# Windowed attention on one core: crossed projection stripes, one-bank reads, 192-byte copies of x, and 14 or 13 units in turn on VectorE

## The chip, the cores and the metric

The kernel runs on one core of a Trainium2 chip. The metric is the device time of one execution in microseconds (us). Times of the kernel before: median 968.16 us of 3 runs (967.62 to 971.61).

## The reference, cut to what matters

The input is an image x of 224 x 224 positions with 96 channels in bf16. It is multiplied with one weight to q, k and v. The first 48 channels attend inside horizontal stripes of 8 rows, the last 48 inside vertical stripes of 8 columns. Both parts go through one output weight.

```python
qkv = jnp.einsum('bhwc,cd->bhwd', x, wqkv)            # 96 -> 3 * 96
q, k, v = qkv[..., :C], qkv[..., C:2 * C], qkv[..., 2 * C:]
scale = C2 ** (-0.5)                                  # C2 = 48, sw = 8
qh = q[..., :C2].reshape(B * nh, sw * W, C2)          # 28 stripes of 1792 positions
...
ah = _softmax(jnp.einsum('bqc,bkc->bqk', qh, kh) * scale, axis=-1)
oh = jnp.einsum('bqk,bkc->bqc', ah, vh)
...                                                   # the same by columns: av, ov
return jnp.einsum('bhwc,cd->bhwd', o, wo)             # o = oh in channels 0..47, ov in 48..95
```

## The kernel before, in words

Two stripes are worked on together; such a pair is called P. Pairs 0 to 13 are horizontal, 14 to 27 vertical. Of the two stripes one (w = 0) lies in partitions 0 to 63 of every tile and the other (w = 1) in 64 to 127. TensorE's array is used as four corners of 64 x 64: a matmul that reads partitions 0 to 63 and writes partitions 64 to 127 uses another corner than one that reads and writes 0 to 63.

**Units.** The 1792 queries of a pair are cut into chunks of 512, 512, 512 and 256 (CH). For each chunk the 1792 keys are gone through in units: a unit has 128 keys and 512 queries, or 256 keys and 256 queries in the last chunk. So a pair has 14 + 14 + 14 + 7 = 49 units. For a unit, `qk` (L752) makes the scores of both stripes in two PSUM banks, reading and writing the same half of the partitions. Then the exponential is taken in one of two ways:

- on ScalarE (`add_a`, L791): one ACTIVATE over both banks, 1024 columns, to a PT buffer; the two banks have to be neighbours;
- on VectorE (`add_d`, L809): one TENSOR_SCALAR over both banks writes 16-bit integers whose bits, read as bf16, are a coarse exponential (I_sb). Two units share a buffer. Usually two shifted copies are added (U_sb and E_sb, L825), on GpSimd or, where the order says `u`, on VectorE, and the three together correct the coarse form. One group in each pair (QUAD, the sixth, two units) is corrected by masks and a product instead (L813, L814 on VectorE; G_sb, L818, on GpSimd, or on VectorE where the order says `p`).

`ndc` and ND = ["4432"] say how many units of each chunk go to VectorE: 4, 4, 3 and 2, which is 13 of 49; 36 go to ScalarE.

`pv` (L775) multiplies the weights with V, which carries columns of ones, so that the sum of the weights comes along. One product for a ScalarE unit, three for a VectorE unit, two in the corrected group. It writes the other half of the partitions than it reads (`at`), and so uses the two corners that `qk` leaves alone. A chunk collects in one PSUM bank and is then copied to OT_sb on VectorE (L846).

**Projection.** `fin` multiplies OT_sb with the output weight, in groups of up to five blocks. In horizontal pairs (L664, groups in HB) it reads one half and writes the other, as `pv` does. In vertical pairs (L694, groups in VB) both matmuls of a step read the same half of OT_sb, and write both halves. VectorE takes the reciprocal of the sums (L649) and multiplies; horizontal results are kept in Ph_sb (L669), vertical ones go to tmp (L698), are added to Ph_sb on GpSimd (L703), and 16 stores a pair bring them out (`added`, SyncE).

**Loading x.** `blocks` (L407) copies a pair's part of x inside HBM to `x_blocks`, in runs of 64 channels (128 bytes), four copies a pair: two halves of the channels times two stripes. `load` (L414) then transposes it into xa_sb and xb_sb by two DMA transposes, and `prep` makes q, k and v of the next pair (L525, L605). The copies of pairs 1, 2 and 3 are issued at the start; in pair P follow the copies for P + 4 and the transposes for P + 2. All of these DMAs are issued from SyncE.

**The order.** It is written out by hand, outside the kernel's loops. Each operation is put into a stream with a letter (`wk.add`), and the string SEQ says letter by letter which stream's next operation comes: A an exponential on ScalarE, a and b scores, c, d and D products with V, j a read on VectorE, f and e the next pair's projection and its evacuations, g and r those of the output, o the copy to OT_sb, U and P work of GpSimd, u and p the same on VectorE, X and x the copies and loads of x, y a store. BANK gives the PSUM bank of each new tile in the same way. `Work.run` walks SEQ and notes each operation's semaphore waits; `emit` writes each engine's part of it in that order.

Of the kernel before, what the change touches and what calls it, by code (L numbers as in the profile page):

```python
# [19 lines left out]
ND = ["4432"]  # L20
QUAD = [(5,)]
SIDE = [""]
# [6 lines left out]
def diag(P, c):  # L29
    return str(c) in SIDE[P % len(SIDE)]  # L30


SEQ = (
    "HiIxIihIiHiIhiiiihIiHXiiihIiiIixhhxhhxhxhxihxHhxihhhHhxhhhxehHhxehHhxHfexeeaaxaeAbbxajbbAxccfxjbccbXaajbUAXbXj"
    "acacaAaUefAefacacebAcbcuaadadjcAaVcfAeaacUbcbAdacjacddAbdbdadaudadAjfVacccAdbdbedadjadadAbcaxDDDbADaDjaUDaDDAa"
    "oddbcbcAdaxjdaUddAdadadbdbAgajcaccUAcadaxdrdbrAbdxadjadaDxDAUcaccxcbAbcacxjacacADaxDfDtDAaxDaDefcUcxcAefcacace"
    "fAaodddaUdeAdadadefdtDAacacaecPacADaDfDdaAkcefPccceffAcfcadaucaeAgkacPcrcrfffADaDefffkcaegaAcacrcracXcAcaPcbbo"
    "ddAdadajVddAgbbDDrDjXbbDVccacacjAcacacUccArbcbgodXdajacacXAacUcdXrbdrAdbdaXjdadgAXdaUdaDrDbrAbDDajcacfAccaUcac"
    "ebdAXbddajdadfAdacacUecbDAbDaDjaDfcXAcacacUeXcaAcacbXboddAdadXjadfdUdAdadaedbDAbeDaDajDfcAkcaUdadedaAdacbgbcAc"
    "jcaUdadcAacraDrbDbDAcajcaUDfcAcacaecfcAcaceacfkcfAtcaaaodddfkAdadefdfdfAdaeDaDbDbtAgacacjPcADacaccrcaArUgbcard"  # L40
# [24 lines left out]
    "DjaccAUaaodddbdbADaXDjaDfDAdXUdacaecXAbcbcacjaXcfcAacUaccegAaraodddbrdAbdadajUdadAdadfDDaADegbDacUrcbArcacajdf"
    "dAdadacecaUAdaegbdrDbrDAacacjfDDAckacakcekcbAbcacjacacAcacaccuaAbboddUddAjdadaDaDAdagbdbrDUArdadaDjcacAcacfddA"
    "uadadbdebdAcajcaccfADaDaDeDacaAcbtcbcfjcfAcfcacacAceaUaccaaodAddadatdfdfAdbpdbDfDAjDaPDaccAcaegaUcrcArffcfacaX"
    "cePgaAcbrcarbDDAdVajdacccAcacaXcbubcAcajacVccAacaoddbdAbdaDjaDfXDAUdadaXDecbAcbXcacjacfcXAcUacacegAacaroddadAr"
    "dadbUdbgAdjadaddDADarDarUDbcbAcajcacfdAcacaceUcbAbdadjadfdAdcacaDeaDAUaDebDbcfcAjcacaccAcakecUagcrcAarabodddbd"
    "AdajdakdfdkAdadaDeDbAbDaDjacfcUcAcadaedadAadbDbgDAjUcacaddAcarcarDaDaAccbtcbcfjcfAcacacfcAcaeUcacaaAoddadadtdf"  # L70
    "AdfdfpdaDaADbeDPbDcjAfcfcacaUcfAceXgacacrbdPrbAdacajgcAacVaccrcArcaXcabDubDAcacajcaVcAcacoddbdAbdXaDjaDfDAXUda"
    "daceXcbADbcacXjacfcAcUcaacegAcaarodddrfAdadaUdbedbADaDjaDfDdAdadaecbUcbAecacjagcAdadadrdbrkAdbUdajDaDfDAcaDace"
    "acAcakcbugbcAcarcjkaccAccacarcacaAbUoddbddAjdadadfdADaDeaDUbDbAdadjacfccAdadaedbUdbAcagjaddAcacacrcarADDatDbDb"
    "AfcftcacacfjcAPcaacccAecaPaccaaAoddadadPdfAdfdfdbebcAUDaDjaDfDfcfAacPaXcedadAacbgbuccrAjcVaacccAcarcaXgUcArcar"
    "caDbDAcbacjacccVAcaaXodddbAdbXDajDadfAUdXaDaDceXbcAbcacjacfcAcUacaccegAaaoddadrdaArgUdbdrdbrAdadjadfDADaDaDecb"
    "UcAbcacjacfcAdadadedaAUacebcbdfdAjDDaDaDAckcaeUgacbcrAbcracacjcAcacackacUAaoddbdbdjdAadadfddAkdaegaDDrArfDaDac"
    "efcfAUcfcaedadbAdbdajdadDAffUcacacfcaAeDaDbDbcfAjcaccacffAcaXceacactacAbcbctAodddaPdadjdAdaXgadVDArDarDaDbcbcA"
    "caucajcPcAcaXcacacAagXpbdbdrcXuAcajcaVcXDAcacarDbcbcAUacjacaccAaodddbdbADaDjaDfUDAdadacecbAcbcajaccfcAUacacceg"
# [106 lines left out]
class Work:  # L185
# [63 lines left out]
    def emit(s, eng, name):  # L249
        known = {}  # L250
        for waits, op in s.out[name]:
# [9 lines left out]
            op.fn(eng).then_inc(op.wait[0], 16 if op.dma is not None else 1)  # L261


HB = [0, 5, 10, 15, 20, 24, 28]
VB = [0, 5, 10, 14]


def bass_standalone__window_attn_cswin__vision_kernel(
# [8 lines left out]
    SW = 8  # L277
# [633 lines left out]
```

## Time and profile before

The profiled execution took 970.69 us. Its span is 968.9 us, the rest lies around it.

| | before |
|---|---|
| median of 3 runs | 968.16 us |
| profiled execution / its span | 970.69 / 968.9 us |
| mean granted clock of TensorE | 0.996 |
| GpSimd busy | 724.3 us, 75% |
| DMA, mean over the span | 65 GB/s |
| HBM read, written | 25.32 MB, 34.41 MB |

In the lines of the profile, PE is TensorE's matmuls, PEld its weight loads, DVE VectorE, ACT ScalarE, POOL GpSimd and SP SyncE, whose DMA issues stand as SPq. L775 is line 775 of the kernel. A group's line has the operation, output<-input with shapes, how often, then busy us and mean ns of one, then the idle time ahead of it and what ended it. A timeline's line has the start, the length, the operation and how many of it are merged; in brackets stands idle time and what ended it. The name behind "waited for" is the instruction whose end released the waiting one.

### The profile page before, as it was taken

The numbers are of one execution on the slowest core, as the hardware profiler recorded it, in microseconds if no ns is written. First come the engines' busy times: TensorE is split into PE (matmuls) and PEld (weight loads), VectorE is DVE, ScalarE is ACT, GpSimd is POOL, SyncE is SP. The second block draws the span as 40 slices with busy tenths as digits, with TensorE's granted clock in tenths as the row PEclk, the third lists the DMA queues.
The fourth block names the chain that finished last, engine by engine and source line by source line (L and its number), as shares of the span: only waits on it lengthen the run. The fifth ranks groups of instructions, "written<-read, shape, count | busy, mean of one in ns | idle before, by whom it ended". The sixth has DMA issues, their size and how long they took to land.

```text
span 968.9 us, 46993 instructions
## 1 busy us (share of the span) xinstructions
PE 956.6 (99%) x21130; PEld 651.4 (67%) x21130; DVE 893.7 (92%) x1426; ACT 942.6 (97%) x1017; POOL 724.3 (75%) x537
## 2 busy tenths in 40 slices
PE   8999999999999999999999999999999999999997
PEld 4667666767666676667677766777776677667674
DVE  7789999999899999999989999999999999999994
ACT  6989999999999999999999999999999999999996
POOL 4778768767966867887778787878777877777772
PEclk9999999999999999999999999999999999999999
DMA  7965234414541553355135345435652631231102
GB/s 120 164 106 79 32 49 79 70 21 71 78 69 14 78 73 46 42 79 79 38 44 80 73 65 79 80 60 85 97 92 47 84 68 33 45 65 32 29 14 50
DMA packets 355098, 63.22 MB, mean 65 GB/s; under 512 B 354784, under 2 KB 354784, under 8 KB 354896
## 3 DMA queue, kind: packets, MB, share of 16 engines
q1 hardware_dynamic: 353312, 59.67, 40.1%
q8 instruction: 165, 2.70, 1.2%
q10 hardware_dynamic: 1584, 0.55, 0.2%
q14 instruction: 37, 0.30, 0.1%
HBM read 25.32 MB, written 34.41 MB: 62 GB/s over the span
## 4 chain that ended last, share of the span: by engine, by line
PE 97%; DVE 2%; ACT 1%; issue 1%; ACTq 0%; DVEq 0%
PE ps L775 51%; PE ps L752 33%; PE ps L525 5%; PE ps L605 4%; PE ps L694 2%; PE ps L664 1%; DVE I_sb L809 1%; ACT PT L791 1%; PE ps L388 0%; DVE KT_sb L545 0%; DVE out_sb L708 0%; PE ps L486 0%; DVE U_sb L813 0%; DVE tmp L698 0%; DVE E_sb L814 0%
## 5 line engine op out<-in xcount | busy, mean ns | idle before, releaser
L791 ACT ACTIVATE PT<-ps 128x1024 bf16<-128x1024 f32 x1008 | 938.5, 1039 | 12.0 <-PE ps L752 8.5
L752 PE MATMUL ps<-QT_sb,KT_sb 48*64 48x512 bf16 (+1 forms) x6272 | 762.4, 357 | 3.7 <-issue 2.0
L775 PE MATMUL ps<-PT,V_sb 64*50 64x512 bf16 (+1 forms) x4592 | 517.2, 351 | 0.0
L809 DVE TENSOR_SCALAR I_sb<-ps 128x1024 int16<-128x1024 f32 x364 | 444.5, 1222 | 31.0 <-PE ps L752 18.1
L752 PEld LDWEIGHTS ps<-QT_sb,KT_sb 48*64 48x64 bf16 x6272 | 275.0, 105 | 164.3 <-ACT PT L791 62.0
L775 PEld LDWEIGHTS ps<-PT,V_sb 64*50 64x50 bf16 x4592 | 238.7, 100 | 39.7 <-ACT PT L791 0.5
L825 POOL TENSOR_SCALAR U_sb<-I_sb 128x2048 int16<-128x2048 int16 (+1 forms) x121 | 213.3, 1763 | 63.8 <-DVE I_sb L809 37.8
L825 POOL TENSOR_SCALAR E_sb<-I_sb 128x2048 int16<-128x2048 int16 (+1 forms) x126 | 224.5, 1782 | 42.6 <-PE ps L775 18.9
L775 PE MATMUL ps<-U_sb,Vs_sb 64*50 64x512 bf16 (+1 forms) x1344 | 195.4, 359 | 0.0
L775 PE MATMUL ps<-I_sb,V_sb 64*50 64x512 bf16 (+1 forms) x1344 | 190.0, 360 | 0.2
L775 PE MATMUL ps<-E_sb,Vs_sb 64*50 64x512 bf16 (+1 forms) x1344 | 175.7, 359 | 0.0
L703 POOL TENSOR_TENSOR out_sb<-tmp,Ph_sb 128x480 bf16<-128x480 f32 (+1 forms) x84 | 85.8, 1027 | 32.0 <-DVE tmp L698 9.4
L818 POOL TENSOR_TENSOR G_sb<-I_sb,U_sb 128x512 bf16<-128x512 bf16 x58 | 66.0, 1154 | 46.6 <-DVE E_sb L814 34.4
L620 POOL TENSOR_SCALAR Vs_sb<-V_sb 128x1400 bf16<-128x1400 bf16 x56 | 76.0, 1358 | 22.3 <-DVE U_sb L825 5.6
L775 PEld LDWEIGHTS ps<-U_sb,Vs_sb 64*50 64x50 bf16 x1344 | 73.7, 100 | 18.6
L846 DVE CAST OT_sb<-ps 128x512 bf16<-128x512 f32 x112 | 69.4, 619 | 15.5 <-PE ps L775 14.0
L775 PEld LDWEIGHTS ps<-E_sb,Vs_sb 64*50 64x50 bf16 x1344 | 71.9, 100 | 14.0
L775 PEld LDWEIGHTS ps<-I_sb,V_sb 64*50 64x50 bf16 x1344 | 68.4, 100 | 14.8 <-ACT PT L791 1.2
L525 PE MATMUL ps<-xa_sb,w_sb 48*64 48x512 bf16 (+3 forms) x440 | 77.5, 351 | 0.1
L525 PE MATMUL ps<-xb_sb,w_sb 48*64 48x512 bf16 (+2 forms) x436 | 75.8, 349 | 0.0
L539 DVE TENSOR_SCALAR QT_sb<-ps 128x512 bf16<-128x512 f32 (+1 forms) x111 | 68.5, 618 | 3.0 <-PE ps L525 1.4
L545 DVE TENSOR_SCALAR_CACHE_REDUCE KT_sb<-ps 128x512 bf16<-128x512 f32 x110 | 67.6, 617 | 0.9 <-PE ps L525 0.8
(66 smaller groups left out, 918.4 us busy)
## 6 DMA issues: line engine op xcount, KB each, us to landing
x_blocks<-in_x_dram SPq DMA_DIRECT2D x106, 224.0 KB
out_dram<-out_sb SPq DMA_DIRECT2D x208, 42.0 KB, 2.1
out_dram<-out_sb SPq DMA_DIRECT2D x22, 24.0 KB, 1.9
xa_sb<-x_blocks SPq DMA_TRANSPOSE x27, 5.1
xb_sb<-x_blocks SPq DMA_TRANSPOSE x27, 5.4
Ph_sb<-in_x_dram ACTq DMA_DIRECT2D x1, 336.0 KB, 3.2
x_blocks<-in_x_dram SPq DMA_DIRECT2D x2, 168.0 KB
out_dram<-out_sb ACTq DMA_DIRECT2D x6, 24.0 KB, 1.9
```

Of the source, the lines that this page charges most:

```text
L525: ins = e.matmul(out_, lhsT=wt, rhs=rhs, start=i == 0, stop=startup or i == 1)
L539: return e.tensor_scalar(dst, src, QS, None, ALU.mult)
L545: return e.tensor_scalar(dst, src, 1.0, None, ALU.mult, ALU.add, accum_out=acc)
L620: vs_ready.setdefault(P, []).append(wk.add("V", Op("pool", 1.4, lambda e, i=i: e.tensor_scalar(Vs_sb[b][i][:, :, :].rearrange("p k c -> p ...
L703: return lambda e, bk: e.tensor_tensor(out_sb[b][:, k0:k1, w, :], tmp[t][:, s0:s1, :], Ph_sb[:, k0:k1, j0 + w, :], ALU.add)
L752: ins = e.matmul(bank(t.k)[64 * w:64 * w + 64, i * qs:(i + 1) * qs], lhsT=KT_sb[b][64 * w:64 * w + C2, 64 * k:64 * k + 64], rhs=QT_sb[b][6 ...
L775: ins = e.matmul(bank(k_.slot.k)[at(P, c, w):at(P, c, w) + CP, 0:qs], lhsT=V_[64 * w:64 * w + 64, k, :], rhs=rhs()[64 * w:64 * w + 64, h * ...
L791: a = wk.add("A", Op("act", ACT, lambda e: e.activation(split(PT[i % NPT]), two(ts), ACTF.Exp, scale=LN128), qs_ + pt_free.get(i - NPT, [] ...
L809: ds.append(wk.add("j", Op("dve", 1.13, lambda e, ts=ts, j=j: e.tensor_scalar(split(I_sb[y], 1024 * j), two(ts), one, 0.0, ALU.add, ALU.ma ...
L818: return lambda e: e.tensor_tensor(G_sb[l][:, i0:i1], I_sb[y][:, i0:i1].bitcast(BF16), U_sb[y][:, i0:i1].bitcast(BF16), ALU.mult)
L825: fn = lambda e, dst=dst, c=c: e.tensor_scalar(dst[:, 0:m], I_sb[y][:, 0:m], float(c), 1.0, ALU.add, ALU.mult)
L846: k.evac = wk.add("o", Op("dve", 0.07 + qs / 960, lambda e, k=k, b=P % 2, q0=q0, qs=qs: e.tensor_copy(OT_sb[b][:, q0:q0 + qs], bank(k.slot ...
```

## The change

- ND becomes two strings, used in turn: pairs with an even number keep 13 units on VectorE, pairs with an odd number get 14 (4, 4, 4, 2). ScalarE's exponentials go from 1008 to 994.
- A unit on VectorE is read by two TENSOR_SCALARs of 512 columns, one for each bank, in place of one of 1024; each gives its bank back by itself, and the two banks need not be neighbours.
- The output projection is cut otherwise. In horizontal pairs the 28 steps are two kinds: 13 pair different blocks of the two stripes such that a matmul reads and writes the same half (the corners of the scores), 15 write the other half. In vertical pairs all steps read and write the same half, except in the last pair. Ph_sb, out_sb and the stores follow that layout, with 24 stores a pair in place of 16. `fin_pe` holds all of a pair's projections, and tmp has three buffers in place of four.
- A pair's copy of x keeps all 96 channels of a stripe together (192 bytes), two copies a pair in place of four; the two transposes overlap by 64 channels, and the weights w2_sb have zeros where a channel is not wanted, so that a projection contracts 64 rows in place of 48. At the start only the copies of pairs 1 and 2 are issued; in pair P follow the transposes for P + 2 and then the copies for P + 3.
- `diag`, `at` and the SIDE table go (SIDE was empty).
- SEQ and BANK are other strings. SEQ has 11213 letters in place of 10740: j 756 in place of 364, u 80 in place of 89, p 36 in place of 27, y 334 in place of 230.

```diff
-ND = ["4432"]
+ND = ["4432","4442"]
...
-HB = [0, 5, 10, 15, 20, 24, 28]
-VB = [0, 5, 10, 14]
+HB = [[0, 4, 9, 13], [0, 5, 10, 15]]
+VB = [0, 5, 10, 15, 20, 24, 28]
...
-            for h in range(2):
-                for w in range(2):
-                    j = 2 * P + w if is_h[P] else 2 * (P - NPH) + w
...
+            for w in range(2):
+                j = 2 * P + w if is_h[P] else 2 * (P - NPH) + w
+                at = j * (NTOK if is_h[P] else SW) * C
+                runs, steps = ([[C, NTOK]], [[CX, NTOK]]) if is_h[P] else ([[C, SW], [W * C, H]], [[H * CX, SW], [CX, H]])
+                dst = bass.AP(xs.tensor, xs.offset + P * NTOK * CX + C * w, steps + [[1, C]])
+                src = bass.AP(x.tensor, x.offset + at, runs + [[1, C]])
...
-                src = bass.AP(xs.tensor, xs.offset + (2 * P + h) * NTOK * 128, [[128, NTOK], [1, 128]])
+                src = bass.AP(xs.tensor, xs.offset + P * NTOK * CX + 64 * h, [[CX, NTOK], [1, 128]])
...
-                                o = at(P, bc // 8, w)
-                                ins = e.matmul(bk3[64 * w:64 * w + 64, s, :], lhsT=OT_sb[b][o:o + CA, bc * 64:(bc + 1) * 64],
-                                               rhs=wo_sb[0][o:o + CA, :], start=True, stop=True)
+                                o, to = 64 - 64 * w, 64 * w if kind else 64 - 64 * w
+                                blk = 2 * (i0 + s) + (w ^ kind) if i0 + s < 13 else 13 + i0 + s
+                                ins = e.matmul(bk3[to:to + 64, s, :], lhsT=OT_sb[b][o:o + CA, blk * 64:(blk + 1) * 64], rhs=wo_sb[0][o:o + CA, :], start=True, stop=True)
...
-                            o = at(P, k // 4, w)
-                            for p0 in (0, 64):
-                                ins = e.matmul(bk3[p0:p0 + 64, s, :], lhsT=OT_sb[b][o:o + CA, 128 * k + p0:128 * k + p0 + 64], rhs=wo_sb[1][o:o + CA, :], start=True, stop=True)
+                            for h in range(2):
+                                to = 64 - 64 * h
+                                o, blk = (64 - 64 * wf, 2 * (i0 + s) + (to > 0)) if final else (to, (i0 + s) ^ h)
+                                ins = e.matmul(bk3[to:to + 64, s, :], lhsT=OT_sb[b][o:o + CA, 64 * blk:64 * blk + 64], rhs=wo_sb[1][o:o + CA, :], start=True, stop=True)
...
-                ds.append(wk.add("j", Op("dve", 1.13, lambda e, ts=ts, j=j: e.tensor_scalar(split(I_sb[y], 1024 * j), two(ts), one, 0.0, ALU.add, ALU.max),
-                                         qs_ + (y_free.get(n - NY, []) if j == 0 else []), lat=1.22, give=ts)))
+                for h, t in enumerate(ts):
+                    at = 1024 * j + 512 * h
+                    ds.append(wk.add("j", Op("dve", 0.6, lambda e, t=t, at=at: e.tensor_scalar(I_sb[y][:, at:at + 512], bank(t.k), one, 0.0, ALU.add, ALU.max),
+                                             [qs_[h]] + (y_free.get(n - NY, []) if at == 0 else []), lat=0.69, give=[t])))
...
-            if P + 4 < NP:
-                blocks(P + 4, "X")
             if P + 2 < NP:
                 load(P + 2, "X")
+            if P + 3 < NP:
+                blocks(P + 3, "X")
```

More of the change, by code (lines that the diff above doesn't have):

```diff
@@ L651, in fin, with pe_fn @@
             if is_h[P]:
-                for i0, i1 in zip(HB[:-1], HB[1:]):
-                    if not q0 < 64 * i1 <= q0 + qs:
-                        continue
-                    g = list(range(i0, i1))
-                    n = len(g)
+                todo = [(kind, i0, i1) for kind in range(2) for i0, i1 in zip(HB[kind][:-1], HB[kind][1:]) if q0 < min(128 * i1, NTOK) <= q0 + qs]
+                for kind, i0, i1 in todo:
+                    n = i1 - i0
                     r = len(held_rc) % NR
-                    def pe_fn(e, bk, g=g, n=n):
+                    def pe_fn(e, bk, n=n, i0=i0, kind=kind):
@@ L672, in fin @@
                                   [("dve", 0.095, lambda e, bk, n=n, r=r: d1(e, bk, r, n), ring(held_rc, NR), True, "r"),
-                                   ("dve", 0.07 + 0.1 * n, d2, [], True, "r")],
-                                  mode="s" if len({diag(P, bc // 8) for bc in g}) > 1 else "q" if diag(P, g[0] // 8) else "v", steps=n)
+                                   ("dve", 0.07 + 0.1 * n, d2, [], True, "r")], mode="v" if kind else "q", steps=n)
                     held_rc.append([ops[-1]])
-                    fin_pe[P] = [p]
+                    fin_pe[P].append(p)
@@ L725, in fin @@
                     added[P].append(ops[-1])
-                    if last:
-                        for s, (w, k) in enumerate(wk_):
-                            store("act" if s % 2 else "sp", k, w, [ops[1 + s]])
-                    elif P == NP - 1:
-                        for w, k in wk_:
-                            store("act" if c == NCH - 2 and w else "sp", k, w, ops[-1:])
-                    elif len(added[P]) == 2 * (len(VB) - 1):
+                    if final:
+                        for s in range(n):
+                            store("act" if (s if last else wf and c == 2) else "sp", i0 + s, wf, ops[1 + s:2 + s] if last else ops[-1:])
+                    elif len(added[P]) == len(VB) - 1:
@@ L738, in bass_standalone__window_attn_cswin__vision_kernel, with qk @@
         added = {P: [] for P in range(NP)}
-        def qk(u, stream):
+        def qk(u, stream, pair=True):
             P, c, kts = u
@@ L754, in fn, with pv @@
                     return ins
-                ops.append(wk.add(stream, Op("pe", S, fn, [k_early[P] if kts[-1] < 2 else k_ready[P], q_ready[(P, c)]], steps=len(kts), take=[t], book=[] if h else ts[1:], mode="q")))
+                ops.append(wk.add(stream, Op("pe", S, fn, [k_early[P] if kts[-1] < 2 else k_ready[P], q_ready[(P, c)]], steps=len(kts), take=[t], book=ts[1:] if pair and not h else [], mode="q")))
             last_qk[P][stream] = ops[1]
             return ops, ts
-        def pv(u, stream, ts, rhs, deps, vk=None):
+        def pv(u, stream, ts, rhs, deps, vk=None, pair=True):
             P, c, kts = u
@@ L770, in fn @@
                     me = k_.ops[n]
-                    hh = h if ts[0].k < ts[1].k else 1 - h
+                    hh = 1 - h if pair and ts[0].k > ts[1].k else h
                     th = [2 * kts[0] + hh] if len(kts) == 1 else [2 * kts[hh], 2 * kts[hh] + 1]
@@ L778, in fn @@
                     return ins
-                o = wk.add(stream, Op("pe", S, fn, [deps[h]] + vs, take=[k_.slot], mode="q" if diag(P, c) else "v", steps=len(kts)))
+                o = wk.add(stream, Op("pe", S, fn, [deps[h]] + vs, take=[k_.slot], mode="v", steps=len(kts)))
                 k_.ops.append(o)
```

381 lines of the change are left out of this document (186 added, 195 removed).

## Prediction

> **What bounds the kernel now.** I read the page's first part and its chain first, then the middle of the run by windows, then the groups by form, then the waits, and last the timelines of TensorE, VectorE and ScalarE.
>
> ```profile
> PE 956.6 (99%) x21130; PEld 651.4 (67%) x21130; DVE 893.7 (92%) x1426; ACT 942.6 (97%) x1017; POOL 724.3 (75%) x537
> PE 97%; DVE 2%; ACT 1%; issue 1%; ACTq 0%; DVEq 0%
> ```
>
> The chain runs along TensorE nearly all the time, but matmuls overlap, so the 99% says little. ScalarE is as full. Which of them sets the pace is seen in the steady stretch:
>
> ```profile
> 15.00:40.00 25.00, 24.92 (x409) 14.20 (x411) 21.43 (x33) 24.18 (x26) 18.09 (x11) 1.00 1.03 156
> 40.00:45.00 5.00, 4.72 (x205) 4.01 (x195) 4.48 (x10) 4.61 (x6) 4.08 (x6) 1.00 1.30 177
> 45.00:50.00 5.00, 3.27 (x41) 2.21 (x43) 1.30 (x3) 2.48 (x3) 4.16 (x4) 0.71 0.92 159
> 50.00:60.00 10.00, 10.00 (x208) 7.36 (x199) 9.31 (x13) 7.42 (x8) 6.69 (x4) 0.98 1.08 170
> 60.00:940.00 880.00, 879.28 (x19759) 602.10 (x19754) 830.44 (x1311) 877.08 (x945) 678.18 (x494) 1.00 0.39 60
> ```
>
> After the length come PE, PEld, DVE, ACT and POOL, then the granted clock, the DMA share and GB/s. From 60 to 940 us ScalarE runs 945 exponentials in 880 us, one each 0.931 us. A pair of stripes has 36 of them, so a pair takes 33.52 us, and there are 28. VectorE is busy 830.44 of the 880, that is 31.63 us in each pair. Before 60 us something else is wrong (below).
>
> ```profile
> L791 ACT ACTIVATE PT<-ps 128x1024 bf16<-128x1024 f32 x1008 | 938.5, 1039 | 12.0 <-PE ps L752 8.5
> ```
> ```profile
> 399.42 12.98 ACT L791 ACTIVATE PT<-ps 128x1024 bf16<-128x1024 f32 x14
> ```
>
> Fourteen exponentials in a row last 12.98 us; one takes 1.04 us (1039 ns), so thirteen steps take 11.94, 0.919 each. A pair cannot be shorter than 36 x 0.919 = 33.1 us on ScalarE. It is at 98.7% of what it can do.
>
> ```profile
> 399.68 0.38 PE L775 MATMUL ps<-PT,V_sb 64*50 64x512 bf16 x2
> 399.84 0.38 PE L752 MATMUL ps<-QT_sb,KT_sb 48*64 48x512 bf16 x2
> 399.90 0.38 PE L775 MATMUL ps<-PT,V_sb 64*50 64x512 bf16 x2
> 400.05 0.38 PE L752 MATMUL ps<-QT_sb,KT_sb 48*64 48x512 bf16 x2
> 400.12 0.38 PE L775 MATMUL ps<-PT,V_sb 64*50 64x512 bf16 x2
> ```
>
> Scores (L752) use one diagonal of the four 64x64 corners of the array, values (L775) the other, and the two run side by side: each repeats after 0.215 us (399.68, 399.90, 400.12; 399.84, 400.05), and neither slows the other. So TensorE is two lanes. A unit needs two steps on the score lane. On the value lane it needs two steps if ScalarE made its weights, six if VectorE made them with three terms, four in the pair's two corrected units. A pair of 13 VectorE units needs 36 x 2 + 11 x 6 + 2 x 4 = 146 value steps, 31.4 us. The output projection of a pair is 28 steps of 97 columns, 28 x 97/512 x 0.215 = 1.1 us, and before the change it also occupies the value lane. That is 32.5 of 33.5 us: the value lane is the second bound, at 97%. The score lane has 98 steps, 21 us, plus the projections of the next pair, and is slack.
>
> **The change part by part.** *One more VectorE unit in every other pair.* Fourteen exponentials go (1008 to 994): at 0.931 each 13.0 us, which is the whole gain if ScalarE keeps its present pace, 0.47 us in a mean pair. On the value lane each moved unit adds four steps, 0.86 us, or 0.43 in a mean pair.
>
> *Crossed stripes.* In the first 14 pairs 13 of 28 projection steps go to the score lane (0.5 us off the value lane); in the other 14 (but the last) all go there, and the pairs of matmuls no longer share their rows (1.1 us off).
>
> ```profile
> L694 PE MATMUL ps<-wo_sb,OT_sb 49*64 49x97 bf16 x784 | 36.8, 206 | 0.6 <-DVE OT_sb L846 0.5
> L664 PE MATMUL ps<-wo_sb,OT_sb 49*64 49x97 bf16 x784 | 31.5, 205 | 0.0
> ```
>
> Both forms keep their 784 matmuls. A mean pair's value lane is then 31.4 + 0.43 + 1.1 - 0.8 = 32.1 us: 0.4 less, so the lane makes room for the new unit and keeps its 97% at about 33.1. What they gain is lost if the score lane has no free slot there; at 21 us plus some 5 for projections it has.
>
> *Reads bank by bank.* 364 reads of 1024 columns become 756 of 512. The nearest rows:
>
> ```profile
> L809 DVE TENSOR_SCALAR I_sb<-ps 128x1024 int16<-128x1024 f32 x364 | 444.5, 1222 | 31.0 <-PE ps L752 18.1 <-PE ps L775 1.8 <-POOL out_sb L703 0.4
> L846 DVE CAST OT_sb<-ps 128x512 bf16<-128x512 f32 x84 | 57.7, 687 | 13.1 <-PE ps L775 11.9
> ```
> ```profile
> 400.75 0.69 DVE L846 CAST OT_sb<-ps 128x512 bf16<-128x512 f32 x1 [0.38 <-PE ps L775]
> 401.36 1.21 DVE L809 TENSOR_SCALAR I_sb<-ps 128x1024 int16<-128x1024 f32 x1
> ```
> ```profile
> 408.55 1.22 DVE L809 TENSOR_SCALAR I_sb<-ps 128x1024 int16<-128x1024 f32 x1
> 409.68 0.65 DVE L610 CAST V_sb<-ps 128x480 bf16<-128x480 f32 x1
> ```
>
> With work queued behind it, a 512-column read occupies VectorE for 0.61 us (400.75 to 401.36) and a 1024-column one for 1.13 (408.55 to 409.68); the rest of the shown duration, about 0.08, lies under the next instruction. Two halves cost 1.22, so 0.09 more: 13 x 0.09 = 1.2 us a pair. The extra unit adds 1.22 in every other pair, 0.6. If each half is late and VectorE stands between them, it pays the full 0.687: the other end, 2 x 0.687 - 1.13 = 0.24 a unit, 3.2 us a pair. I take 0.09, since that row has the same columns and the same kind of source. [...]
>
> The order also moves work between VectorE and GpSimd: 36 products of 1024 on VectorE in place of 27, 80 shifts in place of 89; about +0.1 us a pair, and GpSimd, at 75%, gets nine more shifts and eighteen fewer products and stays hidden. VectorE needs 31.63 + 1.2 + 0.6 + 0.1 = 33.5 us in a mean pair as the page counts busy. That count holds 0.08 of tail at every stop; 1311 instructions with all tails hidden would be up to 1311/880 x 33.52 x 0.08 = 4 us less. The need lies between 29.5 and 33.5. Semaphores and the reciprocals' followers keep some tails, so I take the upper half of it, about 32.5. VectorE goes from the slack engine to the tightest of three.
>
> What the reads give: the first bank comes free 0.6 us earlier, and no neighbouring pair of banks is needed.
>
> ```profile
> PEld ps L752 <- ACT PT L791: 62.0, 264, 0.5
> PEld ps L752 <- DVE I_sb L809: 33.0, 126, 1.0
> DVE I_sb L809 <- PE ps L752: 18.1, 56, 0.6
> ```
>
> Score weights wait for VectorE to free banks 126 times, 33.0 us, and VectorE in turn waits 18.1 us for scores. Halves shorten both, at most 33 us if all were on the path, and nothing if they fall into the score lane's slack. This, not a lower VectorE load, is what can let VectorE run nearer to full.
>
> So a pair: ScalarE 35.5 x 0.919 = 32.6, value lane 32.1, VectorE about 32.5. Three queues at one height, each waiting for the others through eight banks, do not reach it: now the highest alone, 33.1, gives 33.52. I take 33.2, that is 0.32 x 27 = 8.6 us less; bounds 13 less (ScalarE keeps 0.931) and nothing (33.5).
>
> *Copies of x in 192-byte rows, half as many, one pair later.*
>
> ```profile
> q1 hardware_dynamic: 353312, 59.67, 40.1%
> q8 instruction: 165, 2.70, 1.2%
> x_blocks<-in_x_dram SPq DMA_DIRECT2D x106, 224.0 KB
> ```
> ```profile
> 44.35 0.38 PE L752 MATMUL ps<-QT_sb,KT_sb 48*64 48x256 bf16 x3
> 46.73 0.30 PE L752 MATMUL ps<-QT_sb,KT_sb 48*64 48x256 bf16 x2 [2.00 <-issue]
> 47.49 0.84 PE L752 MATMUL ps<-QT_sb,KT_sb 48*64 48x256 bf16 x3
> ```
> ```profile
> 44.41 1.02 ACT L791 ACTIVATE PT<-ps 128x1024 bf16<-128x1024 f32 x1 [0.39 <-PE ps L752]
> 47.16 1.02 ACT L791 ACTIVATE PT<-ps 128x1024 bf16<-128x1024 f32 x1 [1.73 <-PE ps L775]
> 48.86 1.02 ACT L791 ACTIVATE PT<-ps 128x1024 bf16<-128x1024 f32 x1 [0.67 <-PE ps L752]
> 50.85 1.02 ACT L791 ACTIVATE PT<-ps 128x1024 bf16<-128x1024 f32 x1 [0.96 <-PE ps L752]
> 53.03 1.94 ACT L791 ACTIVATE PT<-ps 128x1024 bf16<-128x1024 f32 x2 [1.16 <-PE ps L752]
> ```
>
> From 15 to 60 us the DMA engines are full (share 0.92 to 1.30, later 0.39): before the change the copies for three pairs, in 128-byte rows, are all issued ahead. At 44.35 TensorE stops for 2.0 us for no semaphore ("issue"), then runs at half speed (clock 0.71 from 45 to 50). Five exponentials that start 44.41 to 53.03 span 8.62 us where four steps need 3.7: 4.9 us lost. Code arrives by DMA too (q8), so I read it as code that came late behind the copies. After the change a pair copies 2 x 1792 rows and not 4 x 1792, and only two pairs' are ahead. With the queues free the stop should go: I take 4.0 us of the 4.9, with ends 0 and 6 (the start's other small gaps). [...]
>
> Stores go from 16 to 24 a pair on SyncE's queue; DMA at 0.39 hides them, and the end of the program keeps its shape. If loads fell behind stores on that queue, the next pair's projection would start late; the transposes are placed a whole pair ahead. The 64 contracted rows in place of 48 change no column count: nothing.
>
> **Sum.** 8.6 + 4.0 = 12.6 us less. The profiled execution took 970.7 us (span 968.9), 2.5 above the median of 968.16. From it 958.1; against the median, 955.6. I say 956.
>
> **The rivals.** *VectorE is the bound at once* (0.2): its need is the 33.5 as counted, tails and all, the pair gains at most 0.1, and only the start improves: 968 - 2 - 4 = 962, to 967 with the stop still there. For it: three small sums all add to VectorE. Against: it stood still 50 us of 880.
>
> *Half reads stop between the halves* (0.1), the slower side: the second half's scores are not ready, every half costs 0.687, a pair needs 31.63 + 3.2 + 0.7 + 0.1 = 35.6, less 1 us for tails counted already: 34.6, 1.1 above now. 27 x 1.1 - 4 = 26 us: 994. It decides when more than about a third of the 27 halves pay in full, for then VectorE passes 33.5; half-way there gives 977. Against: only 56 of 364 reads wait for scores today.
>
> *ScalarE alone stays the bound* (0.12): the banks do what they should, all 13 us come, and the stop goes: 968.2 - 13 - 6 = 949, at best 946.
>
> *The lanes do not free* (0.03): projections in the score lane push scores back and the extra unit lands on a full value lane: 33.5 + 0.1 a pair, 967.
>
> **How the numbers follow.** The forecast itself (948 to 962) gets 0.55. Half a per cent, 4.8 us, is about what can be told from no change: below 963.3 is faster. Faster: 0.55 + 0.12 + 0.08 of the first rival = 0.75. Same: the other 0.12 of it and 0.03, 0.15. Slower: 0.10. The range reaches from 946 to 967 and leaves out the slow rival and some of each edge.
>
> **What would show it.** Right: exponentials x994 at about 0.935 us from 60 us on; VectorE at 96 to 98% busy in the steady windows; reads x756 with 0.61 us from start to start; no "issue" stop and clock 1.00 in the second pair; DMA share near 0.3; the waits of scores for VectorE's reads down from 33.0. Wrong: VectorE near 100% with ScalarE's idle growing (first rival); reads with VectorE idle between two halves (second); the stop still there with the DMA share low, which would mean that copies were not its cause.

## The result, and the profile after

The changed kernel takes 953.8 us (median of 4 runs, 953.66 to 955.23); the kernel before took 969.42 beside it (4 runs, 967.62 to 971.61). The ratio is 0.9841, with a 95% interval of 0.9815 to 0.9867: 15.4 us or 1.6% faster. The profiled execution took 953.67 us, its span is 951.6. The forecast was 956, from 946 to 967. Beside the experiments 27 of 41 executions of the kernel before took 966.9 to 969.2 us and 14 took 970.0 to 971.2, and the profiled one of 970.69, in which the clock falls to 0.71 from 45 to 50 us, is like the 14.

The page's first part and its chain, of the kernel after:

```profile
span 951.6 us, 47764 instructions
PE 941.0 (99%) x21298; PEld 644.4 (68%) x21298; DVE 910.6 (96%) x1818; ACT 929.8 (98%) x1003; POOL 735.2 (77%) x528
PE 97%; DVE 1%; DMA 1%; ACT 0%; issue 0%; DVEq 0%; ACTq 0%
```

VectorE went from 92% to 96% and ScalarE from 97% to 98%. "issue", 1% of the chain before, is at 0%. The windows, with the same columns and limits as before:

```profile
15.00:40.00 25.00, 24.92 (x498) 14.48 (x498) 23.42 (x45) 22.98 (x25) 19.19 (x14) 1.00 0.76 127
40.00:45.00 5.00, 5.00 (x142) 4.01 (x140) 4.72 (x9) 4.93 (x6) 3.65 (x4) 1.00 0.57 64
45.00:50.00 5.00, 5.00 (x132) 3.74 (x122) 4.75 (x12) 4.98 (x7) 4.76 (x4) 1.00 0.99 169
50.00:60.00 10.00, 10.00 (x192) 5.51 (x190) 9.95 (x25) 10.00 (x13) 8.99 (x5) 1.00 0.35 49
60.00:940.00 880.00, 879.72 (x20147) 607.94 (x20143) 853.01 (x1687) 876.92 (x944) 693.49 (x490) 1.00 0.34 57
```

Two things are to be seen. From 60 to 940 us ScalarE still runs one exponential in 880/944 = 0.932 us, though a pair now has 35.5 of them in the mean and not 36: 33.09 us. VectorE is busy 853.01 of the 880 us, 96.9%, and idle 27 us where it was idle 49.6. And the clock is 1.00 from 40 to 60 us, with ScalarE full, where it was 0.71 and 0.98 before. The two groups:

```profile
L777 ACT ACTIVATE PT<-ps 128x1024 bf16<-128x1024 f32 x994 | 925.8, 1045 | 6.4 <-PE ps L738 3.5
L797 DVE TENSOR_SCALAR I_sb<-ps 128x512 int16<-128x512 f32 x756 | 487.4, 680 | 7.4 <-PE ps L738 3.7
```
The exponentials' idle time fell from 12.0 to 6.4 us, and the reads' from 31.0 to 7.4. The waits:

```profile
PEld ps L738 <- ACT PT L777: 59.5, 255, 0.6
PEld ps L738 <- DVE I_sb L797: 15.2, 63, 0.5
DVE I_sb L797 <- PE ps L738: 3.7, 14, 0.5
```

Scores waited 126 times and 33.0 us for VectorE's reads; it is 63 times and 15.2 us now, and VectorE waits 3.7 us for scores in place of 18.1. The score lane's wait for ScalarE hardly moved (62.0 and 59.5).

**Where the time went.** The last chunk of a pair ends with a copy to OT_sb of 256 columns. In VectorE's timeline, its start in the first and in the last pair, first of before, then of after:

```profile
54.62 0.42 DVE L846 CAST OT_sb<-ps 128x256 bf16<-128x256 f32 x1
961.66 0.42 DVE L846 CAST OT_sb<-ps 128x256 bf16<-128x256 f32 x1 [1.80 <-PE ps L775]
```
```profile
48.45 0.38 DVE L834 CAST OT_sb<-ps 128x256 bf16<-128x256 f32 x1
942.86 0.42 DVE L834 CAST OT_sb<-ps 128x256 bf16<-128x256 f32 x1 [0.38 <-PE ps L761]
```

The first pair ends 6.2 us earlier. The 27 pairs after it take 894.41 us in place of 907.04: 12.6 less, 33.13 a pair in place of 33.59. From the last copy to the end of the span it is 8.7 us in place of 7.2: 1.5 more. The sum is -17.3, the difference of the spans (968.9 and 951.6).

Two other profiles say how firm these parts are. Experiment 12 is in effect a repeat of the changed kernel: its first pair ends at 49.51, its 27 pairs take 896.80 us (33.21 a pair), and the end takes 7.4, so the pairs give 10.2 to 12.6 us and the end costs 0.2 to 1.5. In experiment 10, an edit of the kernel before with the same copies in which the clock does not fall, the first pair ends at 52.46 (one of its exponentials is 0.42 us shorter there). Without the fall of the clock the start therefore gives 3.0 to 4.0 us and not 6.2.

### The profile page after: what moved, and what is told of

It reads as the page before. It is cut to its first block, busy times and chain, and to the rows that moved or that the text cites. A ratio compares the mean times of both kernels' runs of the same rounds, so it can differ in the third digit from the quotient of the medians.

```text
span 951.6 us, 47764 instructions
## 1 busy us (share of the span) xinstructions
PE 941.0 (99%) x21298; PEld 644.4 (68%) x21298; DVE 910.6 (96%) x1818; ACT 929.8 (98%) x1003; POOL 735.2 (77%) x528
## 2 busy tenths in 40 slices
DMA packets 253254, 57.06 MB, mean 60 GB/s; under 512 B 252936, under 2 KB 252936, under 8 KB 253048
## 4 chain that ended last, share of the span: by engine, by line
PE 97%; DVE 1%; DMA 1%; ACT 0%; issue 0%; DVEq 0%; ACTq 0%
PE ps L761 50%; PE ps L738 35%; PE ps L518 5%; PE ps L598 5%; PE ps L653 1%; PE ps L687 1%; DMA w_sb<-in_wqkv_dram 1%; ACT PT L777 0%; DVE I_sb L797 0%; DVE V_sb L603 0%; DVE KT_sb L538 0%; DVE out_sb L698 0%; DVE KT_sb L550 0%; DVE OT_sb L834 0%; PE ps L595 0%
## 5 line engine op out<-in xcount | busy, mean ns | idle before, releaser
L777 ACT ACTIVATE PT<-ps 128x1024 bf16<-128x1024 f32 x994 | 925.8, 1045 | 6.4 <-PE ps L738 3.5
L761 PE MATMUL ps<-PT,V_sb 64*50 64x512 bf16 (+1 forms) x4536 | 496.3, 350 | 0.0
L797 DVE TENSOR_SCALAR I_sb<-ps 128x512 int16<-128x512 f32 x756 | 487.4, 680 | 7.4 <-PE ps L738 3.7
L738 PEld LDWEIGHTS ps<-QT_sb,KT_sb 48*64 48x64 bf16 x6272 | 279.7, 105 | 156.6 <-ACT PT L777 59.5
L813 POOL TENSOR_SCALAR E_sb<-I_sb 128x2048 int16<-128x2048 int16 (+1 forms) x135 | 245.9, 1821 | 36.0 <-DVE U_sb L813 18.3
L813 POOL TENSOR_SCALAR U_sb<-I_sb 128x2048 int16<-128x2048 int16 (+1 forms) x121 | 223.6, 1848 | 45.6 <-DVE I_sb L797 19.6
L761 PEld LDWEIGHTS ps<-PT,V_sb 64*50 64x50 bf16 x4536 | 226.4, 100 | 37.6
L761 PE MATMUL ps<-E_sb,Vs_sb 64*50 64x512 bf16 (+1 forms) x1456 | 170.7, 352 | 0.0
L518 PE MATMUL ps<-xa_sb,w_sb 64*64 64x512 bf16 (+3 forms) x440 | 78.1, 353 | 0.3 <-DMA w_sb<-in_wqkv_dram 0.3
L518 PE MATMUL ps<-xb_sb,w_sb 64*64 64x512 bf16 (+2 forms) x436 | 75.7, 348 | 0.0
L806 POOL TENSOR_TENSOR G_sb<-I_sb,U_sb 128x512 bf16<-128x512 bf16 x40 | 45.2, 1154 | 30.1 <-DVE E_sb L802 21.4
```

The lines of the kernel that those rows point to most:

```text
L518: ins = e.matmul(out_, lhsT=wt, rhs=rhs, start=i == 0, stop=startup or i == 1)
L738: ins = e.matmul(bank(t.k)[64 * w:64 * w + 64, i * qs:(i + 1) * qs], lhsT=KT_sb[b][64 * w:64 * w + C2, 64 * k:64 * k + 64], rhs=QT_sb[b][6 ...
L761: ins = e.matmul(bank(k_.slot.k)[64 - 64 * w:64 - 64 * w + CP, 0:qs], lhsT=V_[64 * w:64 * w + 64, k, :], rhs=rhs()[64 * w:64 * w + 64, h * ...
L777: a = wk.add("A", Op("act", ACT, lambda e: e.activation(split(PT[i % NPT]), two(ts), ACTF.Exp, scale=LN128), qs_ + pt_free.get(i - NPT, [] ...
L797: ds.append(wk.add("j", Op("dve", 0.6, lambda e, t=t, at=at: e.tensor_scalar(I_sb[y][:, at:at + 512], bank(t.k), one, 0.0, ALU.add, ALU.ma ...
L813: fn = lambda e, dst=dst, c=c: e.tensor_scalar(dst[:, 0:m], I_sb[y][:, 0:m], float(c), 1.0, ALU.add, ALU.mult)
```

## The experiments

All times are medians with the lowest and highest run; where a kernel is an edit of the changed one, its distance is taken from 953.8 us. The last experiment is in effect a repeat of that kernel and took 955.15, 1.4 us more, so distances under 2 us say little, and the larger ones are uncertain by that much.

**1. The kernel before, with the copies of x for pairs 2 to 5 cut to 8 rows.** Their transposes read pair 1's rows.

```diff
+                    rows = 8 if 2 <= P <= 5 else NTOK
-                    runs, steps = ([[C, NTOK]], [[128, NTOK]]) if is_h[P] else ...
+                    runs, steps = ([[C, rows]], [[128, rows]]) if is_h[P] else ...
-                src = bass.AP(xs.tensor, xs.offset + (2 * P + h) * NTOK * 128, ...)
+                src = bass.AP(xs.tensor, xs.offset + (2 * (1 if 2 <= P <= 5 else P) + h) * NTOK * 128, ...)
```

> The kernel before, with the copies of x for pairs 2 to 5 cut to 8 rows each; these pairs transpose the blocks of pair 1 again, so their part of the output is left out. All other work and the order are unchanged. Theory (the DMA engines, full of copies until 60 us, held back TensorE's code): the stop at 44 us and the half clock behind it go, DMA share from 15 to 60 us falls from about 1.05 to below 0.7, and the time falls by 4 to 6 us, to about 963. Rival (TensorE ran out of code because its instructions are dense there, whatever the DMAs do): the stop stays, the time stays within 1.5 us of 968.

Measured: 967.36 us (966.21 to 967.97, 10 runs) beside 970.23 of before (15 runs), ratio 0.9977 (0.9966 to 0.9988). TensorE's timeline and the windows of this kernel, at the place of the stop:

```profile
44.35 0.38 PE L753 MATMUL ps<-QT_sb,KT_sb 48*64 48x256 bf16 x3
44.97 0.30 PE L753 MATMUL ps<-QT_sb,KT_sb 48*64 48x256 bf16 x2 [0.24 <-issue]
```
```profile
40.00:45.00 5.00, 4.76 (x209) 4.06 (x202) 4.48 (x10) 4.61 (x6) 4.09 (x6) 1.00 0.02 5
45.00:50.00 5.00, 5.00 (x121) 4.48 (x123) 4.04 (x6) 3.79 (x5) 4.55 (x5) 1.00 0.99 127
```

The same two groups of matmuls that stood 2.4 us apart before (44.35 and 46.73) are now 0.6 apart, with the DMA share at 0.02 in place of 1.30, and the clock does not drop. So the stop does hang on the copies. That it is code that TensorE waits for is borne out by the queue of instructions, q8: in the traces of the kernel before and of experiments 2, 3, 10 and this one, a packet of q8 is counted at 44.1, 43.85, 44.6, 43.55 and 42.35 us, and TensorE goes on at 46.73, 46.42, 47.20, 46.25 and 44.97, each time 2.5 to 2.7 us behind it. With the copies cut, the packet came 1.75 us earlier and TensorE went on 1.76 earlier.

In this kernel the first pair ends at 51.19 and the last one's copy starts at 958.19: 3.4 us come at the start, and the 27 pairs take 907.0 us as before. The ratio gives 2.2 us (with an interval of 1.2 to 3.3). Both hold, the ratio in part, the fall of the clock as well, and that does not always follow the stop. From experiment 10, the stop and the window behind it:

```profile
46.25 0.30 PE L752 MATMUL ps<-QT_sb,KT_sb 48*64 48x256 bf16 x2 [1.32 <-issue]
```
```profile
45.00:50.00 5.00, 3.75 (x91) 3.33 (x95) 2.93 (x6) 3.62 (x4) 4.37 (x4) 1.00 1.00 181
```

Against that profile the copies are worth 1.3 us (52.46 and 51.19), against the one with the fall of the clock 3.4. What decides whether the clock falls is not shown: in experiment 3 TensorE stands 2.07 us and the clock stays at 1.00.

**2. The kernel before, with bank-by-bank reads alone.** Its order stays, each j twice.

```diff
+                for h, t in enumerate(ts):
+                    at = 1024 * j + 512 * h
+                    ds.append(wk.add("j", Op("dve", 0.6, ... tensor_scalar(I_sb[y][:, at:at + 512], bank(t.k), ...), [qs_[h]] ..., give=[t])))
-        wk.run(SEQ, BANK)
+        wk.run(SEQ.replace("j", "jj"), BANK)
```

> The kernel before, with one part of the change alone: VectorE reads each score bank by its own instruction of 512 columns and gives it back by itself; units, order of everything else, projection and copies as before. VectorE gets 364 x 0.08 = 29 us more work. Theory (VectorE has slack and the early return of a bank shortens TensorE's waits): the time changes by less than 4 us either way; VectorE's busy share in the steady stretch rises from 94% to about 97%. Rival (each half stops between banks and pays 0.687): 20 to 30 us slower. Second rival (the reads are where the gain comes from): 5 us or more faster.

**3. The kernel before, each read cut into two instructions inside one operation.** Both banks come back at its end, as before.

```diff
+                def read(e, ts=ts, j=j):
+                    for i, k in enumerate(sorted(t.k for t in ts)):
+                        ins = e.tensor_scalar(I_sb[y][:, at:at + 512], bank(k), ...)
+                    return ins
+                ds.append(wk.add("j", Op("dve", 1.13, read, ..., give=ts)))
```

> The kernel before, with the read of 1024 columns cut into two instructions of 512 that start together when both banks are ready, both banks given back behind the second: the price of the halves without their use. Theory (0.08 us a unit more, both halves back to back): VectorE's reads go from 0.61 us start to start; the time rises by 0 to 10 us, and by at least 2 us more than in the run where each bank is given back by itself, because the first bank comes free half a read later there. Rival (the early return is worth nothing): both runs take the same time within 1.5 us.

Measured, on one chip: 965.32 us (964.5 to 966.29, 4 runs) with the banks given back one by one, ratio 0.9955 (0.9938 to 0.9971); 982.02 us (981.34 to 983.9, 4 runs) with both at the end, ratio 1.0129 (1.0111 to 1.0148). The waits of the one, then of the other:

```profile
PEld ps L752 <- DVE I_sb L811: 7.3, 27, 0.5
DVE I_sb L811 <- PE ps L752: 5.0, 16, 0.6
```
```profile
PEld ps L752 <- DVE I_sb L812: 56.1, 187, 1.1
DVE I_sb L812 <- PE ps L752: 16.6, 50, 0.7
```

Both kernels issue the same 728 reads. The cut by itself costs 12 us. Taking each bank by itself is worth 16.7 us (982.02 - 965.32), and the score lane's wait for VectorE is 7.3 us in the one and 56.1 in the other. The two kernels differ in two things: in the first, a read also starts as soon as its own bank's scores are there, while the second waits for both banks (VectorE's wait for scores is 5.0 and 16.6). How the 16.7 us divide between the earlier start and the earlier return was not tried. Alone, in an order that was not made for it, the edit brings 4 to 5 us by the medians and 3.2 in the 27 pairs (903.87 for 907.04).

**4. The changed kernel, with all projections but the last pair's on the value lane**, as none of them crossed.

```diff
-                                o, to = 64 - 64 * w, 64 * w if kind else 64 - 64 * w
+                                o, to = 64 - 64 * w, 64 * w
-                                ... else (to, (i0 + s) ^ h)
+                                ... else (64 - to, (i0 + s) ^ h)
```

> The changed kernel, with all output projections but the last pair's put on the value lane (they read one half and write the other, so blocks land in wrong places of the output); same count of matmuls, same order. Theory (the value lane is at 97%, and what was moved to the score lane made room): 13 pairs x 28 steps + 14 x 13 steps = 546 steps of 0.041 us = 22 us more on that lane, of which half or more shows: 964 to 976 us. Rival (the lanes' crossing is worth nothing, the projection fits anywhere): within 3 us of 953.8.

Measured: 973.4 us (973.17 to 973.64, 6 runs), 19.6 above the changed kernel, and slower than the kernel before: 1.0038 (1.0024 to 1.0052). The edit moves 13 x 14 + 28 x 13 = 546 steps of 0.041 us (an estimate: 97 columns of the 512 that take 0.215), 22 us, to the other lane. Nearly all of it shows. Without the crossing, this order with its additional units and one-bank reads would have lost time. (The order was made for the crossing, and in the vertical pairs of the kernel before each step used one corner of either lane, so this is not the old projection.)

**5 to 9. The changed kernel with work added to one engine or lane at a time**, spread over the run. The added work is computed and thrown away (5, 6), or a step is done twice (7 to 9); an added exponential or read also keeps its bank that much longer. Priced with nothing waiting, a one-bank exponential takes 0.49 us (in the fifth kernel's timeline one starts at 194.19 and the next exponential at 194.68), a read 0.60, a step 0.215.

```diff
+                if i % 20 == 10:                         # 5: 50 exponentials of one bank, ScalarE
+                    e.activation(junk[:, :], bank(ts[0].k), ACTF.Exp, scale=LN128)
+                        if i % 20 == 10:                 # 6: 38 reads of one bank, VectorE
+                            e.tensor_scalar(junk[:, :], bank(t.k), one, 0.0, ALU.add, ALU.max)
+                    m = 2 if n % 40 == 20 and me is not k_.first and me is not k_.end else 1    # 7: product steps
+                    m = 2 if n == 10 and me is not k_.first and me is not k_.end else 1         # 9: the same, at another index
+                    for i, k in enumerate(th * m):
+                def fn(e, t=t, th=th, m=2 if len(scored) % 26 == 13 else 1):                    # 8: score steps
+                    for i, k in list(enumerate(th)) * m:
```

> The changed kernel with 50 extra exponentials of one bank (512 columns, about 0.48 us each, into a buffer that nobody reads), one ahead of every twentieth exponential: 24 us more on ScalarE and on nothing else. Theory (ScalarE, the value lane and VectorE stand at one height): most of it shows, 18 to 25 us, to 972 to 979 us. Rival (VectorE alone sets the pace since the change): under 10 us.

> The changed kernel with 38 extra reads of one bank on VectorE (0.60 us each, into a buffer that nobody reads), one ahead of every twentieth read: 23 us more on VectorE and on nothing else. Theory (three at one height; VectorE stands still 27 of 880 us): 10 to 20 us show, 964 to 974. Rival (ScalarE alone sets the pace, VectorE fits beside it): under 6 us.

> The changed kernel with about 110 steps of products with V done twice (0.215 us each; the output of those chunks is wrong by the doubled terms): 23 us more on the value lane. Theory (three at one height): 10 to 20 us show. Rival (since the crossed stripes the value lane has room): under 6 us.

> The changed kernel with 105 steps of scores done twice (0.215 us each, the same result): 23 us more on the score lane. Theory (the score lane is slack, but a late score also holds up its exponential, which stands behind it in order): 0 to 10 us show, less than in each of the other three. Rival (TensorE has no two lanes that matter, only one queue in order): as much as the doubled products.

> The changed kernel with one step of products with V in nearly every chunk done twice (up to 112 steps of 0.215 us, at most 24 us more on the value lane; the output is wrong by the doubled terms). The run before it doubled only 43 steps at most, 9 us, and cost 6.7. Theory (three at one height): 14 to 22 us show. Rival (the value lane has room for a few us and then fills): under 10 us.

The seventh kernel's doubled index was often a chunk's first or last step, which stays single: only 43 more pairs of matmuls came of it, and 28 of them have 256 columns, half a step each. That is 29 steps, 6.2 us in place of some 24, so the ninth repeats it with 84 pairs of 512. The eighth kernel's trace has 90 more pairs of 512 and 32 of 256: 106 steps. Measured:

| added to | work added | median (lowest to highest, n) | ratio to before | above 953.8 |
|---|---|---|---|---|
| ScalarE | 50 exponentials of 512, about 24.5 us | 974.24 (973.37 to 975.66, 4) | 1.0068 (1.0052 to 1.0085) | 20.4, 83% |
| VectorE | 38 reads, 22.8 us | 971.96 (971.05 to 972.34, 4) | 1.0039 (1.0024 to 1.0054) | 18.2, 80% |
| value lane | 29 steps, 6.2 us | 960.45 (959.07 to 961.54, 4) | 0.9920 (0.9906 to 0.9935) | 6.7, 107% |
| value lane | 84 steps, 18.1 us | 966.96 (965.94 to 967.72, 10) | 0.9986 (0.9977 to 0.9996) | 13.2, 73% |
| score lane | 106 steps, 22.8 us | 961.92 (960.86 to 963.35, 4) | 0.9937 (0.9922 to 0.9952) | 8.1, 36% |

No engine alone is the bound: 20 us or so of work on ScalarE, on VectorE and on the value lane show at 73 to 83% each, the three shares sum to well over one, and even the score lane, which has room, passes on a third. (Taken from the repeat's 955.15, the 73 to 83% are 65 to 78%, and the third is 30%. The seventh kernel's 6.7 us are too few for a share: 1.4 us are a fifth of them.) From the kernel with more VectorE work, and from the one with more ScalarE work, the steady window:

```profile
60.00:940.00 880.00, 872.95 (x19822) 589.96 (x19820) 859.26 (x1699) 864.28 (x924) 686.50 (x485) 1.00 0.33 56
```
```profile
60.00:940.00 880.00, 874.15 (x19790) 582.66 (x19784) 843.65 (x1660) 877.44 (x968) 684.95 (x484) 1.00 0.34 56
```

With more work for VectorE, ScalarE loses busy time (864.28 us, 876.92 without), and VectorE itself rises only to 97.6%; with more for ScalarE, VectorE falls to 95.9% (843.65).

**10. The kernel before, with one exponential in 36 over one bank only.** The other bank's weights are left from an earlier unit; ScalarE has 12 us less to do, 28 times the 0.42 us by which such an exponential is shorter (1037 and 618 ns, below).

```diff
+            def fn(e):
+                if i % 36 == 18:
+                    return e.activation(PT[i % NPT][:, 0:512], bank(ts[0].k), ACTF.Exp, scale=LN128)
+                return e.activation(split(PT[i % NPT]), two(ts), ACTF.Exp, scale=LN128)
```

> The kernel before, with one exponential in each pair taken over one bank in place of two (the other half of its weights is left from an earlier unit, so that work is left out): 28 x 0.43 = 12 us less on ScalarE, as much as the fourteen moved units take off it, and nothing added to VectorE or the value lane. Theory (ScalarE was the first bound, the value lane next at 97%): 4 to 10 us faster than before. Rival (ScalarE alone sets the pace): 11 to 13 us faster. Second rival (TensorE alone): under 2 us.

Measured: 968.76 us (966.63 to 970.19, 10 runs) beside 968.24 (19 runs), ratio 0.9999 (0.9989 to 1.001). Nothing came of the 12 us. The groups:

```profile
L795 ACT ACTIVATE PT<-ps 128x1024 bf16<-128x1024 f32 x980 | 916.7, 1037 | 17.8 <-PE ps L752 13.9 <-PE ps L775 1.3
L794 ACT ACTIVATE PT<-ps 128x512 bf16<-128x512 f32 x28 | 17.3, 618 | 0.0
```

The exponentials' idle time, 12.0 us before, rose to 17.8, 13.9 of it for scores: part of what ScalarE was spared it waited for TensorE, and each of the other exponentials kept it busy for 0.935 us in the mean (916.7 over 980) in place of 0.931. The theory, 4 to 10 us, fell. In the kernel before, ScalarE at 98.7% was not what held the pace by itself; its own work could go down by 12 us and the time stayed.

**11. The changed kernel, with 24 more copies at the start**, in rows of 128 bytes to a place that nobody reads, four ahead of each copy of pairs 1 to 3.

```diff
+                    if P in (1, 2, 3):
+                        for n in range(4):
+                            e.dma_start(... [[128, NTOK], [1, 64]], ... [[C, NTOK], [1, 64]]).then_inc(s_junk, 16)
```

> The changed kernel with four extra copies of 1792 rows of 128 bytes issued ahead of each of the six copies of pairs 1 to 3, to a place that nobody reads: 24 more copies in the first 35 us, about as many rows as before the change. Theory (full DMA queues at the start cost 3 us, as the light run showed): 2 to 6 us slower than 953.8, with DMA share about 1 from 15 to 45 us and a stop of TensorE for no semaphore. Rival (the new order alone cured the start): within 1.5 us.

Measured: 963.95 us (963.76 to 965.17, 4 runs), ratio 0.9956 (0.9941 to 0.9971), 10.2 above the changed kernel: more than expected, and for another reason. TensorE's timeline and the window of the start:

```profile
34.59 0.63 PE L527 MATMUL ps<-xa_sb,w_sb 64*64 64x512 bf16 x2 [4.08 <-DMA xb_sb<-x_blocks]
```
```profile
15.00:40.00 25.00, 20.84 (x318) 10.25 (x316) 18.27 (x37) 17.27 (x19) 16.96 (x11) 0.93 0.87 127
```

TensorE stands 4.08 us for a transpose of x that comes late behind the flood, and there is no stop by "issue" up to 60 us. The run shows that full queues cost time at the start; it does not show the late code a second time and says nothing on its price.

**12. The changed kernel, with the 192-byte rows of the horizontal pairs written as two runs of 96.** It was to tell the size of a packet from the number of copies.

```diff
-                runs, steps = ([[C, NTOK]], [[CX, NTOK]]) if is_h[P] else ...
+                runs, steps = ([[C, NTOK], [C2, 2]], [[CX, NTOK], [C2, 2]]) if is_h[P] else ...
```

> The changed kernel with each row of the horizontal pairs' copies cut into two runs of 96 bytes: the packets of these 26 copies double. Theory (outside the start the DMAs are hidden): DMA packets rise by some 45000, the time stays within 1.5 us. Rival (each packet delays TensorE's code or the loads in the steady stretch too): 3 us or more slower.

Measured: 955.15 us (953.35 to 955.8, 4 runs), ratio 0.9860 (0.9845 to 0.9874). The line of the DMA packets is the same in both pages:

```profile
DMA packets 253254, 57.06 MB, mean 60 GB/s; under 512 B 252936, under 2 KB 252936, under 8 KB 253048
```

Neighbouring runs were joined, no packet was cut, and the run says nothing on their size. What it gives is a repeat of the changed kernel.

## Why the prediction was right, and where it was not

**The sign, the size and the mechanism** came as forecast: 953.8 where 956 was said, 14 fewer exponentials at an unchanged pace, room made on the value lane, earlier banks, and a start without the stop. The terms of the sum were off one by one, and in part the number was luck. The 4.0 us of the start were read from the profile of 970.69, with the fall of the clock in them, and taken off a median that is 2.5 us shorter than that profile.

**The pair** was taken as 33.2 us, 8.6 less over 27 pairs; it measured 33.13, 12.6 less, and 33.21, 10.2 less, in the repeat. The step that was too careful is "three queues at one height do not reach it": they came nearer to it than the present pair did, and ScalarE kept its 0.932 us for an exponential, which was the best bound of that step (13 us). VectorE's busy time, an upper bound of its need since it still holds tails, came out at 853.01/880 x 33.09 = 32.1 us a pair, where 33.5 was counted and a need of 32.5 was taken. A read costs what was said or a little less. From VectorE's timeline after:

```profile
405.11 1.88 DVE L797 TENSOR_SCALAR I_sb<-ps 128x512 int16<-128x512 f32 x3
406.90 0.68 DVE L813 TENSOR_SCALAR U_sb<-I_sb 128x2048 int16<-128x2048 int16 x1
```

Three reads from 405.11 to 406.90 are 0.60 each (0.61 was taken). The split by itself cost 12 us (experiment 3: 982.02 beside 970.23). By the rows two reads of 512 columns in place of one of 1024 cost 0.07 us more (2 x 0.60 less 1.13), and against it stand the 16.7 us that taking each bank by itself was worth.

**The first bound** was called ScalarE, at 98.7%, with the value lane second. That reading was wrong as a statement on one engine: experiment 10 took 12 us off ScalarE for nothing. The forecast survived because the change did not rest on it alone. It lowered ScalarE, freed the value lane and shortened the banks' stay together, and experiments 2 to 4 show what each of the last two is worth: 19.6 us hang on the crossing in the changed kernel, 16.7 on taking each bank by itself in the kernel before. What a fourteenth unit alone does to the kernel before was not tried, since it needs another order; experiment 10 argues that it would have brought nothing. Nor was the new order tried by itself.

**"The score lane is slack"** holds in part. Added score steps show at 36% and not at 0. The lane took up the projections for that little; the vertical ones also became shorter, as forecast:

```profile
L687 PE MATMUL ps<-wo_sb,OT_sb 49*64 49x97 bf16 x784 | 31.7, 205 | 0.5 <-DVE OT_sb L834 0.5
```

It was 36.8 us for the same 784 matmuls when two of them shared their rows.

**The start** was taken as 4.0 us (0 to 6) and measured 6.2 against a profile in which the clock falls, 3.0 to 4.0 against one in which it does not. That the stop came from the copies is shown (experiment 1); with the clock at 1.00 their share is 1.3 us, less than the 4 that the prediction put down to them, and with its fall 3.4. The rest, 1.7 to 2.7 us (from 51.19 to 49.51 and 48.45), came with the other parts of the change. In the profile after, the order keeps ScalarE full in the second pair: forty exponentials stand in one stretch (in the repeat a gap of 0.81 us cuts it), where the prediction showed five gaps.

```profile
32.74 37.68 ACT L777 ACTIVATE PT<-ps 128x1024 bf16<-128x1024 f32 x40 [0.32 <-PE ps L738]
```

Which part of the change does it stays open. So the term was nearer to right than its reason. The stop does hang on the copies: with the DMA share at 1.30 the two groups of matmuls stood 2.4 us apart, with 0.02 they stood 0.6 (experiment 1).

**The end** was said to keep its shape, at no cost. It took 1.5 us more in the profile after and 0.2 more in the repeat; what the difference comes from is open.

**The rivals.** VectorE as the bound at once would have left the pair at 33.4: it is 33.13, and VectorE, at 96.9%, is one of three. Reads that stop between their halves are out: the reads' whole wait for scores is 3.7 us. The lanes freed. ScalarE alone as the bound, with all 13 us, is nearest in its number (12.6, and 10.2 in the repeat) and out in its reason, since work added to VectorE or to the value lane shows nearly as much.

## What to carry to other kernels

When several engines are near full, take work away from one or add some to one before you call it the bound: here 12 us off ScalarE, at 98.7%, gave nothing, and 18 to 25 us added to any of three cost 73 to 83% of it. Lower all of them together, and look for what they hold against each other: cutting a read in two cost 12 us, and letting each half wait for and give back its own bank returned 16.7. A lane with slack is the place to move work to, but here it charged for it too: added score steps showed at 36%.

## What the hardware showed that was not expected

- TensorE stopped for a packet of code that came late. In five traces (the kernel before, experiments 1, 2, 3 and 10) it goes on 2.5 to 2.7 us behind a packet of the instruction queue, and with the copies cut that packet came 1.75 us earlier (42.35 us in place of 44.1). With the queues full (share 0.94 to 1.30 from 40 to 45 us) it stood 1.3 to 2.1 us, with a share of 0.02 for 0.24; among the full ones the longest stop had the lowest share, so the share alone does not set its length. Flooded, in a kernel with another order (share 0.87 to 1.20 from 15 to 50 us), a load was late (4.08 us) and no stop by "issue" came up to 60 us. The repeat of the changed kernel has three stops by "issue" of 0.5 to 0.8 us, two of them between 200 and 800 us, so short ones are not bound to the start.
- Two runs of 96 bytes that lie side by side made no more packets than one of 192: 253254 in both forms. Where they are joined, on the chip or ahead of it, is not shown.
- Two matmuls that share their rows of the array were dearer than two that use corners of one diagonal: 36.8 and 31.7 us busy for the same 784, though one by itself takes 206 and 205 ns; the two overlap less.
